# Two window-attention quads in one region of 64x64 products, with the projections of the next quad moved ahead of u and v

## The chip, the cores and the metric

The kernel runs on one core of one Trainium2 chip. The metric is the device time of one execution in microseconds; lower is better. Times of separate executions are compared by their median.

## The reference

The work is the forward and backward pass of windowed self-attention on an image of 256 x 256 tokens with 384 channels, in bf16. The image is cut into 1024 windows of 8 x 8 = 64 tokens, and each window attends only to itself, with a single head over all 384 channels.

```python
qkv = xw @ wqkv                      # xw: (1024, 64, 384)
q, k, v = ...                        # three parts of 384 columns
scale = C ** (-0.5)
p = softmax(einsum('bqc,bkc->bqk', q, k) * scale)
o = einsum('bqk,bkc->bqc', p, v) @ wo
# and with grad_out: the gradients for x, wqkv and wo
```

Inputs are `x`, `wqkv` (384 x 1152), `wo` (384 x 384) and `grad_out`; outputs are the result (`out_0`), the gradient of x (`out_1`), of wqkv (`out_2`) and of wo (`out_3`).

## The kernel before

**Algebra.** The kernel never forms q, k and v. Once, at the start, it multiplies weights: A from the q and k parts (with the scale), B from the v part and wo, and their transposes. After that, for the tokens x and the output gradient g (called `dq` in the code, and `dT` when transposed), it needs four projections: `z` (from g with B), `y` (from x with A), `u` (from x with B, the values that the probabilities average) and `v` (from x with A transposed, for the gradient). Scores and the gradient of the probabilities come from one set of products, `sd`, whose stationary operand is yz.

**Tiling.** Two windows lie on the 128 partitions, and four such pairs make a quad: 512 tokens, 128 quads in all. Every quad goes through these steps:

- `project(a, 0, mo)` and `project(a, 1, mo)` (lines 161 to 173): z and y, three banks each, a bank from three products of 128x128 stationary against 512 columns, evicted by ACT into `yz` (a single buffer). `gather` (lines 175 to 179) copies z, then y, into `zy` on DVE, and `to_tokens` (lines 181 to 184) has SP transpose `zy` by DMA into `tok`.
- `scores(b)` (line 186): 24 products of 64 columns into one PSUM bank, `sd`.
- `soft(b, 0..5)` (lines 198 to 231): softmax and its gradient on DVE, with one exp on ACT (step 2, L212). Step 4 is the last reader of `sd`.
- `uv(b, t, part)` (lines 233 to 241): u and v, eight groups of three products with 384 columns, evicted by ACT.
- `turn(b)` (lines 243 to 259): transposes the two 64x64 matrices of each window on DVE, five instructions. For the first quads and the last one, small products on PE do it.
- `attention(c)` (line 352) calls `attend(c, t)` four times. One `attend` has twelve products in 64x64 mode, in three sets of four that run concurrently on the four quarters of the array: into banks `pw`, `pd`, `pu`, `po`. Their evictions: `Wq` (L294) and `o` (L287) on ACT, `Uq` (L297) on DVE, `d` on DVE or ACT by the table `EV`. A `pd` bank is written by two neighbouring calls, so at t = 0 two of them are taken, and the last one of a quad is the "edge". The results `o` and `d` are stored through POOL's DMA queue.

**Weight gradients.** For every group of three finished quads (`GQ` = 3) there are six items, one for each of two matrices and three row blocks. An item sums over the twelve token blocks of the group and adds the result to `GF_acc` on DVE (L320). An item can be done in two ways. `gf_rows` is a full sum: twelve 128x128 products into one bank `pg`. `gf_halves` is a half sum: 48 products in 64x64 mode into two banks `ph`, cut into twelve slots of four, which `attention` deals out, four behind each `attend`; after twelve slots both banks are added on DVE.

**Order.** The order of instructions on each engine is the order of the program text, written by hand (`manual_schedule`). Tiles, buffers and semaphores are handled by the framework. All PSUM tiles share one ring of eight banks, `ring`; a new tile takes the slot of the tile that was released earliest, and its first product waits for the eviction that released it. `step(c, b, a, ahead)` (line 360) runs three quads at different ages: scores, softmax and u, v of quad b, z and y of quad a = b + 1, a full sum, and then the attention of quad c = b - 1 with one half sum dealt into it. Loads run four quads ahead (`AHEAD`), the DMA transposes of g and x (`load_turn`, L146) two quads ahead; both queues, SP and POOL, work in order.

Of the kernel before, what the change touches and what calls it, by code (L numbers as in the profile page):

```python
# [23 lines left out]
def kernel(  # L24
# [90 lines left out]
    def windows(ap, st, first, count=2):  # L115
        row, col = st["at"]
        return ap[0, row + WIN * first:row + WIN * (first + count), col:col + WIN, :]
# [2 lines left out]
    OTHER = {0: HI, WT: LO}  # L120

    def load_first(st):
        st["xq"] = xq = grp.tile([P, QUAD, C], BF16, tag="xq", name="xq", bufs=2 * GQ + 5)
        st["dq"] = dq = qp.tile([P, QUAD, C], BF16, tag="dq", name="dq", bufs=6)
        for t in range(QUAD):
            (nc.sync, nc.scalar)[t % 2].dma_start(out=dq[:, t, :], in_=windows(grad_out, st, 2 * t))
        nc.sync.dma_start(out=w_sb[:, :, columns(0)], in_=w_in[:, :, columns(0)])
        nc.scalar.dma_start(out=w_sb[:, :, columns(1)], in_=w_in[:, :, columns(1)])
        for t in range(QUAD):
            nc.sync.dma_start(out=xq[:, t, :], in_=windows(x, st, 2 * t))  # L130
        nc.gpsimd.tensor_copy(out=spare[:], in_=dq[:, QUAD - 1, 0:1])

    def load(st):
        st["xq"] = xq = grp.tile([P, QUAD, C], BF16, tag="xq", name="xq", bufs=2 * GQ + 5)
        st["dq"] = dq = qp.tile([P, QUAD, C], BF16, tag="dq", name="dq", bufs=6)
        for t in range(QUAD):
            nc.gpsimd.dma_start(out=dq[:, t, :], in_=windows(grad_out, st, 2 * t))  # L137
        for t in range(QUAD):
            (nc.gpsimd if st["i"] == AHEAD + 1 else nc.sync).dma_start(out=xq[:, t, :], in_=windows(x, st, 2 * t))

    def load_turn(st):
        st["xT"] = qp.tile([P, QUAD, CK, P], BF16, tag="xT", name="xT", bufs=3)
        st["dT"] = qp.tile([P, QUAD, CK, P], BF16, tag="dT", name="dT")
        for src, dst, on_pe in (("dq", "dT", G_ON_PE), ("xq", "xT", X_ON_PE)):
            if st["i"] >= on_pe:
                nc.sync.dma_start_transpose(out=st[dst][:].rearrange("p t m k -> p (t m) k"),  # L146
                                            in_=st[src][:].rearrange("p t c -> p (t c)"))

    def turn_on_pe(st, src, dst):
        for t in range(QUAD):  # L150
# [117 lines left out]
    def attend(st, t):  # L268
        if t == 0:
            st["Uq"] = grp.tile([P, QUAD, C], BF16, tag="Uq", name="Uq")  # L270
            st["Wq"] = grp.tile([P, QUAD, C], BF16, tag="Wq", name="Wq")
        copies = {"A": nc.scalar.copy, "D": nc.vector.tensor_copy}

        def bank(name):
            return ring.tile([P, C], F32, tag="r", name=name)

        def slot(bank, straight, crossed, start=False, stop=False):
            for h in (LO, HI):
                o = OTHER[h.start]
                products = [(h, bank, straight, {"start": True, "stop": True}),  # L280
                            (o, pd[h is LO], crossed, {"start": start, "stop": stop})]
                for o, dst, (lhs, rhs), flags in products if h == LO else products[::-1]:
                    nc.tensor.matmul(dst[o, :], lhsT=operand(st, lhs, t, h), rhs=operand(st, rhs, t, h), **flags)  # L283

        def keep(name, src, i, rows=slice(0, P), sb=None):
            sb = ob.tile([P, C], BF16, tag=name, name=name) if sb is None else sb
            copies[EV[name][i]](out=sb[rows, :], in_=src[rows, :])  # L287
            return sb[rows, :]

        pw = bank("pw")  # L290
        pd = (bank("pd") if t == 0 else st["edge"], bank("pd"))[::-1]
        st["edge"] = pd[0]
        slot(pw, ("Pb", "dq"), ("Pb", "z"), start=True)
        copies[EV["W"][t] if st["i"] >= GQ else "DA"[t % 2]](out=st["Wq"][:, t, :], in_=pw[:])  # L294
        pu = bank("pu")
        slot(pu, ("ST", "xq"), ("dS", "y"))
        copies[EV["U"][t]](out=st["Uq"][:, t, :], in_=pu[:])  # L297
        po = bank("po")
        slot(po, ("PT", "uq"), ("ST", "vq"), stop=True)
        o = keep("o", po, t)  # L300
        above, below = rim.pop("d", None) if t == 0 else None, st["at"][0] + 2 * WIN * QUAD < H
        d = keep("d", pd[1], t, slice(0 if t else WT, P), above)
        nc.gpsimd.dma_start(out=windows(out_0, st, 2 * t), in_=o)  # L303
        if t or above is not None:
            nc.gpsimd.dma_start(out=windows(out_1, st, 2 * t - 1), in_=d if t else above[:])  # L305
        else:
            nc.gpsimd.dma_start(out=windows(out_1, st, 0, 1), in_=d)
        if t == QUAD - 1:
            rim["d"] = sb = ob.tile([P, C], BF16, tag="d", name="d")
            keep("d", pd[0], QUAD, LO, sb)  # L310
            if not below:
                nc.gpsimd.dma_start(out=windows(out_1, st, 2 * QUAD - 1, 1), in_=rim.pop("d")[LO, :])
# [36 lines left out]
                nc.vector.tensor_copy(out=final[f][:, ma, :], in_=GF_acc[:, f, ma, :])  # L349
                yield  # L350

    def attention(st):
        halves = gf_halves(*fill.pop(0)) if fill else iter(())
        for t in range(QUAD):
            attend(st, t)
            yield
            for k in range(QUAD):
                next(halves, None)

    def step(c, b, a, ahead):  # L360

# [40 lines left out]
        for rest in slots:  # L402
            pass

    G_ON_PE, X_ON_PE = 2, 1
    EV = {"z": "AAA", "y": "AAA", "u": "AAAA", "v": "AAAA", "o": "AAAA", "U": "DDDD", "W": "AAAA", "d": "DADAA"}
    quads = [(row, col) for col in range(0, W, WIN) for row in range(0, H, 2 * WIN * QUAD)]
    n = len(quads)
    sts = [{"at": q, "i": i, "on_pe": i <= GQ or i == n - 1} for i, q in enumerate(quads)]
    AHEAD = 4  # L410
    dw_out = out_2.rearrange("(m p) j -> p m j", p=P)
    dwo_out = out_3.rearrange("(m p) n -> p m n", p=P)
# [1 line left out]
    def weight_gradients(group):  # L414
# [19 lines left out]
                copy_out(k, out, pe[:])  # L434

        def rows(name):
            return grp.tile([P, CK, C], BF16, tag="xq", name=name, bufs=2 * GQ + 5)

        for i in range(CK):
            next(group)  # L440
# [26 lines left out]
    with tc.manual_schedule(engines=MANUAL):  # L467
# [5 lines left out]
        load_first(sts[0])  # L473
        load(sts[1])
        load(sts[2])
        load_turn(sts[0])
        load_turn(sts[1])
        load(sts[3])
        load(sts[4])
        turn_blocks(wT[2], w_sb, 2 * CK)  # L480
# [13 lines left out]
        turn_blocks(AT_sb, A_sb)  # L494
        gather(sts[0], 1)
        held = []
        last = None
        get = lambda i: sts[i] if 0 <= i < n else None
        for i in range(n + 1):
            if 0 <= i < n - 2:  # L500
                load_turn(sts[i + 2])
            if 0 <= i < n:
                to_tokens(sts[i])
            step(get(i - 1), get(i), get(i + 1), get(i + AHEAD) if i else None)
            if i > 0:
                held.append(sts[i - 1])
                sts[i - 1] = None
            if held and i == n:
                last = gf_final(held)
            elif len(held) == GQ:  # L510
                fill.extend((held, f, ma) for f in range(2) for ma in range(CK))
                held = []
        while fill:
            gf_rows(*fill.pop(0))
        weight_gradients(last)
# [30 lines left out]
```

## Time and profile before

| what | value |
|---|---|
| median of 3 runs | 1897.86 us (1897.47 to 1898.12) |
| the profiled execution, its own time | 1897.33 us |
| its span, first to last instruction | 1895.6 us |
| granted TensorE clock | 1.0 |
| busy: PE / DVE / ACT / POOL | 1887.7 / 1662.8 / 1523.7 / 862.6 us |
| one steady quad, attention to attention | 14.56 us (905.82 to 920.38) |

In the lines of the profile, "L157" is line 157 of the kernel (the helper that records the products of z, y, u, v, the full sum and the scores, told apart by their tiles pj, pg and sd). PE is the stream of matrix products, PEld the loading of their stationary operands, which overlaps them. A timeline line gives the start and the duration in microseconds, the engine, the line, the operation, the tiles (out <- in), their sizes and how many instructions were merged; in brackets stands the idle time before it and who ended it. A line of the waits gives the engine and line that waited, the one it waited for, the total in microseconds, how many times, and the longest.

### The profile page before, as it was taken

To read this page: it belongs to the slowest core of one execution; us is meant where nothing else is said; L and a number is where in the kernel's file an instruction comes from. 1 tells how busy PE (TensorE), PEld (TensorE's weight loads), DVE (VectorE), ACT (ScalarE), POOL (GpSimd) and SP (SyncE) were. 2 spreads that over 40 slices of the span, in tenths; PEclk is the share of its full clock that TensorE was granted. 3 is DMA by queue.
4 is the path that set the end of the run, shared out by engine and by line. 5 is a ranking of instruction groups with operands and counts; after the bars stand their busy time and mean duration, and the time that the engine had idled before them with its cause. 6 is when DMAs were issued, how large, how long until landed. Compare 5 with 4: busy or idle time off the path is not lost.

```text
span 1895.6 us, 57194 instructions
## 1 busy us (share of the span) xinstructions
PE 1887.7 (100%) x22398; PEld 1125.4 (59%) x22398; DVE 1662.8 (88%) x3602; ACT 1523.7 (80%) x3346; POOL 862.6 (46%) x1576
## 2 busy tenths in 40 slices
PE   9999999999999999999999999999999999999999
PEld 5555565556555655565556555655565566556655
DVE  6888888888888888888888888888888888888887
ACT  7888788878887888788878887888788878887884
POOL 4444444445444444454445444544444445444532
PEclk9999999999999999999999999999999999999999
DMA  9999999999999999999999999999999999999995
GB/s 224 244 212 225 221 211 221 216 221 218 210 222 220 212 224 213 224 215 215 227 215 220 213 218 223 218 208 222 218 222 218 214 222 219 212 213 227 219 183 115
DMA packets 948911, 408.28 MB, mean 215 GB/s; under 512 B 830880, under 2 KB 924064, under 8 KB 948640
## 3 DMA queue, kind: packets, MB, share of 16 engines
q1 hardware_dynamic: 872128, 252.63, 78.2%
q0 software_dynamic: 75264, 151.11, 31.3%
q8 instruction: 175, 2.87, 0.6%
q10 hardware_dynamic: 1248, 0.89, 0.2%
q14 instruction: 96, 0.79, 0.1%
HBM read 101.84 MB, written 101.84 MB: 107 GB/s over the span
## 4 chain that ended last, share of the span: by engine, by line
PE 99%; DVE 1%; ACT 0%; issue 0%; ACTq 0%
PE pj L157 53%; PE pg L157 13%; PE ph L338 13%; PE sd L157 5%; PE pw L283 5%; PE po L283 4%; PE pu L283 4%; PE pd L283 1%; PE pe L427 0%; DVE Uq L297 0%; PE warm L87 0%; PE pc L106 0%; DVE Wq L294 0%; PE pt L99 0%; DVE d L287 0%
## 5 line engine op out<-in xcount | busy, mean ns | idle before, releaser
L303 POOL DMA_DIRECT2D out_dram<-o x512 | 273.6, 534 | 919.3 <-ACT o L287 903.7
L294 ACT CAST Wq<-pw 128x384 bf16<-128x384 f32 x506 | 243.4, 481 | 275.8 <-PE pw L283 275.5
L157 PEld LDWEIGHTS <-xT 128*128 128x128 bf16 x3072 | 291.4, 98 | 182.5
L157 PE MATMUL pj<-B_sb,xT 128*128 128x384 bf16 x1536 | 333.6, 326 | 0.0
L157 PE MATMUL pj<-AT_sb,xT 128*128 128x384 bf16 x1536 | 333.4, 326 | 0.0
L137 POOL DMA_DIRECT2D dq<-in_grad_out_dram x508 | 268.8, 540 | 77.9 <-DMA out_dram<-d 25.2
L297 DVE CAST Uq<-pu 128x384 bf16<-128x384 f32 x512 | 282.8, 552 | 13.8 <-PE pu L283 1.4
L305 POOL DMA_DIRECT2D out_dram<-d x480 | 278.6, 580 | 12.3 <-ACT uq L241 5.1
L157 PE MATMUL pj<-dT,BT_sb 128*128 128x512 bf16 x1152 | 269.6, 379 | 0.1
L157 PE MATMUL pj<-xT,A_sb 128*128 128x512 bf16 x1152 | 269.5, 379 | 0.0
L171 ACT CAST yz<-pj 128x512 bf16<-128x512 f32 x384 | 224.3, 585 | 38.4 <-PE pj L157 29.6
L283 PE MATMUL pd<-tok,ps 64*64 64x384 bf16 x2048 | 254.4, 326 | 0.0
L287 ACT CAST o<-po 128x384 bf16<-128x384 f32 x512 | 250.0, 488 | 1.5 <-PE po L283 1.4
L241 ACT CAST vq<-pj 128x384 bf16<-128x384 f32 x512 | 246.6, 482 | 3.6
L241 ACT CAST uq<-pj 128x384 bf16<-128x384 f32 x512 | 243.7, 476 | 3.7 <-PE pj L157 1.9
L173 ACT CAST yz<-pj 128x512 bf16<-128x512 f32 x384 | 224.7, 585 | 24.5 <-PE pj L157 0.6
L258 DVE STREAM_TRANSPOSE PS<-ps 32x256 bf16<-32x256 bf16 x492 | 214.5, 436 | 9.4
L157 PEld LDWEIGHTS <-xq 128*128 128x128 bf16 x1572 | 153.4, 98 | 115.6 <-issue 0.9
L338 PEld LDWEIGHTS <-xq 64*64 64x64 bf16 x6000 | 175.9, 107 | 67.8
L338 PE MATMUL ph<-Wq,xq 64*64 64x384 bf16 x3984 | 204.2, 323 | 0.0
L157 PEld LDWEIGHTS <-A_sb 128*128 128x128 bf16 x1152 | 112.5, 98 | 135.6
L157 PEld LDWEIGHTS <-BT_sb 128*128 128x128 bf16 x1152 | 112.5, 98 | 122.5
(95 smaller groups left out, 3049.2 us busy)
## 6 DMA issues: line engine op xcount, KB each, us to landing
out_dram<-o POOLq DMA_DIRECT2D x512, 96.0 KB, 3.8
xq<-in_x_dram SPq DMA_DIRECT2D x508, 96.0 KB, 4.0
dq<-in_grad_out_dram POOLq DMA_DIRECT2D x508, 96.0 KB, 5.8
out_dram<-d POOLq DMA_DIRECT2D x480, 96.0 KB, 4.3
out_dram<-d POOLq DMA_DIRECT2D x64, 48.0 KB, 4.8
tok<-zy SPq DMA_TRANSPOSE x128, 7.4
xT<-xq SPq DMA_TRANSPOSE x127, 7.7
dT<-dq SPq DMA_TRANSPOSE x126, 7.7
```

The lines of the kernel that those rows point to most:

```text
L137: nc.gpsimd.dma_start(out=dq[:, t, :], in_=windows(grad_out, st, 2 * t))
L157: nc.tensor.matmul(out, lhsT=lhsT, rhs=rhs, start=start, stop=stop)
L171: ENG[EV["z"][mo]](out=yz[:, mo, :, 0:4:3, :], in_=pj[:])
L173: ENG[EV["y"][mo]](out=yz[:, mo, :, 1:3, :], in_=pj[:])
L241: cp(out=dst[:, t, :], in_=pj[:])
L283: nc.tensor.matmul(dst[o, :], lhsT=operand(st, lhs, t, h), rhs=operand(st, rhs, t, h), **flags)
L287: copies[EV[name][i]](out=sb[rows, :], in_=src[rows, :])
L294: copies[EV["W"][t] if st["i"] >= GQ else "DA"[t % 2]](out=st["Wq"][:, t, :], in_=pw[:])
L297: copies[EV["U"][t]](out=st["Uq"][:, t, :], in_=pu[:])
L303: nc.gpsimd.dma_start(out=windows(out_0, st, 2 * t), in_=o)
L305: nc.gpsimd.dma_start(out=windows(out_1, st, 2 * t - 1), in_=d if t else above[:])
L338: nc.tensor.matmul(dst[o, :], lhsT=st["xq"][h, t, ma * P + o.start:ma * P + o.stop], rhs=st["UW"[f] + "q"][h, t, :], start=(i == 0), stop= ...
```

## The change

Quads 0 to 9 run as before. From quad 10 on, the loop takes two quads at a time (`double(i)`):

- `front(b, a, ...)` runs for each of the two: scores of b, a full sum beside the first softmax steps, then z and y of the next quad a, and only after them u and v of b. In the first front both gathers and the transposition to tokens of a follow at once; in the second they are left for later.
- Then both attentions run one behind the other, each with one half sum dealt out as before. Behind t = 2 and t = 3 of the first attention stand the two gathers of the quad after the pair, and `to_tokens` between the two attentions.
- x of two quads is loaded in the first front, g in each; the transposes of g and x are issued three quads ahead and separately. The x ring has twelve buffers instead of eleven.
- In even quads of the pairs the eviction of `d` at t = 0 goes to ACT instead of DVE.
- The last quad is turned on DVE like the others.

The text of the general case has parameters (`EVEN_ROWS`, `ODD_ROWS`, `EVEN_SETS`), which are all 1 here, so that the branches for no full sum or for two half sums in one attention are taken only where no sums are left.

```diff
--- before.py
+++ after.py
@@ -120,7 +120,7 @@
     OTHER = {0: HI, WT: LO}
 
     def load_first(st):
-        st["xq"] = xq = grp.tile([P, QUAD, C], BF16, tag="xq", name="xq", bufs=2 * GQ + 5)
+        st["xq"] = xq = grp.tile([P, QUAD, C], BF16, tag="xq", name="xq", bufs=2 * GQ + 6)
         st["dq"] = dq = qp.tile([P, QUAD, C], BF16, tag="dq", name="dq", bufs=6)
         for t in range(QUAD):
             (nc.sync, nc.scalar)[t % 2].dma_start(out=dq[:, t, :], in_=windows(grad_out, st, 2 * t))
@@ -130,21 +130,25 @@
             nc.sync.dma_start(out=xq[:, t, :], in_=windows(x, st, 2 * t))
         nc.gpsimd.tensor_copy(out=spare[:], in_=dq[:, QUAD - 1, 0:1])
 
+    def load_dq(st):
+        st["dq"] = dq = qp.tile([P, QUAD, C], BF16, tag="dq", name="dq", bufs=6)
+        for t in range(QUAD):
+            nc.gpsimd.dma_start(out=dq[:, t, :], in_=windows(grad_out, st, 2 * t))
+
+    def load_xq(st):
+        st["xq"] = xq = grp.tile([P, QUAD, C], BF16, tag="xq", name="xq", bufs=2 * GQ + 6)
+        for t in range(QUAD):
+            (nc.gpsimd if st["i"] == AHEAD + 1 else nc.sync).dma_start(out=xq[:, t, :], in_=windows(x, st, 2 * t))
+
     def load(st):
-        st["xq"] = xq = grp.tile([P, QUAD, C], BF16, tag="xq", name="xq", bufs=2 * GQ + 5)
-        st["dq"] = dq = qp.tile([P, QUAD, C], BF16, tag="dq", name="dq", bufs=6)
-        for t in range(QUAD):
-            nc.gpsimd.dma_start(out=dq[:, t, :], in_=windows(grad_out, st, 2 * t))
-        for t in range(QUAD):
-            (nc.gpsimd if st["i"] == AHEAD + 1 else nc.sync).dma_start(out=xq[:, t, :], in_=windows(x, st, 2 * t))
-
-    def load_turn(st):
-        st["xT"] = qp.tile([P, QUAD, CK, P], BF16, tag="xT", name="xT", bufs=3)
-        st["dT"] = qp.tile([P, QUAD, CK, P], BF16, tag="dT", name="dT")
-        for src, dst, on_pe in (("dq", "dT", G_ON_PE), ("xq", "xT", X_ON_PE)):
-            if st["i"] >= on_pe:
-                nc.sync.dma_start_transpose(out=st[dst][:].rearrange("p t m k -> p (t m) k"),
-                                            in_=st[src][:].rearrange("p t c -> p (t c)"))
+        load_dq(st)
+        load_xq(st)
+
+    def load_turn(st, dst):
+        st[dst] = qp.tile([P, QUAD, CK, P], BF16, tag=dst, name=dst, bufs={"xT": 3, "dT": 2}[dst])
+        if st["i"] >= ON_PE[dst]:
+            nc.sync.dma_start_transpose(out=st[dst][:].rearrange("p t m k -> p (t m) k"),
+                                        in_=st[dst[0] + "q"][:].rearrange("p t c -> p (t c)"))
 
     def turn_on_pe(st, src, dst):
         for t in range(QUAD):
@@ -284,7 +288,8 @@
 
         def keep(name, src, i, rows=slice(0, P), sb=None):
             sb = ob.tile([P, C], BF16, tag=name, name=name) if sb is None else sb
-            copies[EV[name][i]](out=sb[rows, :], in_=src[rows, :])
+            ev = EVEN if st["i"] > PAIRED and st["i"] % 2 == 0 and name in EVEN else EV
+            copies[ev[name][i]](out=sb[rows, :], in_=src[rows, :])
             return sb[rows, :]
 
         pw = bank("pw")
@@ -349,13 +354,70 @@
                 nc.vector.tensor_copy(out=final[f][:, ma, :], in_=GF_acc[:, f, ma, :])
                 yield
 
-    def attention(st):
-        halves = gf_halves(*fill.pop(0)) if fill else iter(())
+    def attention(st, sets=1):
+        halves = [gf_halves(*fill.pop(0)) for k in range(min(sets, len(fill)))]
+        slots = (None for part in halves for slot in part)
         for t in range(QUAD):
             attend(st, t)
             yield
-            for k in range(QUAD):
-                next(halves, None)
+            for k in range(QUAD if sets < 2 else QUAD + 2):
+                next(slots, None)
+
+    def front(b, a, rows, gathers):
+        scores(b)
+        soft(b, 0)
+        if rows and fill:
+            soft(b, 1)
+            soft(b, 2)
+            for row in range(rows):
+                gf_rows(*fill.pop(0))
+            z = 0
+        else:
+            z = 2
+            for mo in range(z if a is not None else 0):
+                project(a, 0, mo)
+            soft(b, 1)
+            soft(b, 2)
+        i = b["i"]
+        if a is not None:
+            for mo in range(z, CK):
+                project(a, 0, mo)
+        soft(b, 3)
+        soft(b, 4)
+        soft(b, 5)
+        if i % 2 == 0 and i + AHEAD < n:
+            load_xq(sts[i + AHEAD])
+        if i + AHEAD < n:
+            load_dq(sts[i + AHEAD])
+        if i + 3 < n:
+            load_turn(sts[i + 3], "dT")
+        if a is not None:
+            for mo in range(CK):
+                project(a, 1, mo)
+        if gathers and a is not None:
+            for kind in range(2):
+                gather(a, kind)
+            to_tokens(a)
+        turn(b)
+        if i % 2 == 0 and i + AHEAD + 1 < n:
+            load_xq(sts[i + AHEAD + 1])
+        for t in range(QUAD):
+            for part in range(2):
+                uv(b, t, part)
+        if i + 3 < n:
+            load_turn(sts[i + 3], "xT")
+
+    def double(i):
+        a = sts[i + 2] if i + 2 < n else None
+        front(sts[i], sts[i + 1], EVEN_ROWS, True)
+        front(sts[i + 1], a, ODD_ROWS if a is not None else 2, False)
+        for t, part in enumerate(attention(sts[i], EVEN_SETS)):
+            if t >= 2 and a is not None:
+                gather(a, t - 2)
+        if a is not None:
+            to_tokens(a)
+        for part in attention(sts[i + 1]):
+            pass
 
     def step(c, b, a, ahead):
 
@@ -402,11 +464,14 @@
         for rest in slots:
             pass
 
-    G_ON_PE, X_ON_PE = 2, 1
+    ON_PE = {"dT": 2, "xT": 1}
+    EVEN_ROWS, ODD_ROWS, EVEN_SETS = 1, 1, 1
+    PAIRED = 10
     EV = {"z": "AAA", "y": "AAA", "u": "AAAA", "v": "AAAA", "o": "AAAA", "U": "DDDD", "W": "AAAA", "d": "DADAA"}
+    EVEN = {"d": "AADAA"}
     quads = [(row, col) for col in range(0, W, WIN) for row in range(0, H, 2 * WIN * QUAD)]
     n = len(quads)
-    sts = [{"at": q, "i": i, "on_pe": i <= GQ or i == n - 1} for i, q in enumerate(quads)]
+    sts = [{"at": q, "i": i, "on_pe": i <= GQ} for i, q in enumerate(quads)]
     AHEAD = 4
     dw_out = out_2.rearrange("(m p) j -> p m j", p=P)
     dwo_out = out_3.rearrange("(m p) n -> p m n", p=P)
@@ -434,7 +499,7 @@
                 copy_out(k, out, pe[:])
 
         def rows(name):
-            return grp.tile([P, CK, C], BF16, tag="xq", name=name, bufs=2 * GQ + 5)
+            return grp.tile([P, CK, C], BF16, tag="xq", name=name, bufs=2 * GQ + 6)
 
         for i in range(CK):
             next(group)
@@ -473,8 +538,9 @@
         load_first(sts[0])
         load(sts[1])
         load(sts[2])
-        load_turn(sts[0])
-        load_turn(sts[1])
+        for st in sts[:2]:
+            for dst in ("dT", "xT"):
+                load_turn(st, dst)
         load(sts[3])
         load(sts[4])
         turn_blocks(wT[2], w_sb, 2 * CK)
@@ -494,22 +560,33 @@
         turn_blocks(AT_sb, A_sb)
         gather(sts[0], 1)
         held = []
-        last = None
         get = lambda i: sts[i] if 0 <= i < n else None
-        for i in range(n + 1):
-            if 0 <= i < n - 2:
-                load_turn(sts[i + 2])
-            if 0 <= i < n:
-                to_tokens(sts[i])
+        def done(*quads):
+            for st in quads:
+                held.append(st)
+                sts[st["i"]] = None
+                if len(held) == GQ:
+                    group = held[:]
+                    fill.extend((group, f, ma) for f in range(2) for ma in range(CK))
+                    held.clear()
+
+        for i in range(PAIRED):
+            for dst in ("dT", "xT"):
+                load_turn(sts[i + 2], dst)
+            to_tokens(sts[i])
             step(get(i - 1), get(i), get(i + 1), get(i + AHEAD) if i else None)
-            if i > 0:
-                held.append(sts[i - 1])
-                sts[i - 1] = None
-            if held and i == n:
-                last = gf_final(held)
-            elif len(held) == GQ:
-                fill.extend((held, f, ma) for f in range(2) for ma in range(CK))
-                held = []
+            if i > 0 and i < PAIRED - 1:
+                done(sts[i - 1])
+        for dst in ("dT", "xT"):
+            load_turn(sts[PAIRED + 2], dst)
+        to_tokens(sts[PAIRED])
+        for part in attention(sts[PAIRED - 1]):
+            pass
+        done(sts[PAIRED - 2], sts[PAIRED - 1])
+        for i in range(PAIRED, n, 2):
+            double(i)
+            done(sts[i], sts[i + 1])
+        last = gf_final(held)
         while fill:
             gf_rows(*fill.pop(0))
         weight_gradients(last)
```

## The prediction

> **What bounds the kernel now.** I read the page's busy shares and its chain first, then the waits, then the timelines of PE, DVE and ACT through one step in the middle.
>
> ```profile
> PE 1887.7 (100%) x22398; PEld 1125.4 (59%) x22398; DVE 1662.8 (88%) x3602; ACT 1523.7 (80%) x3346; POOL 862.6 (46%) x1576
> ...
> PE 99%; DVE 1%; ACT 0%; issue 0%; ACTq 0%
> ```
>
> PE is never idle and the chain is PE from end to end. So only two things move the time: PE work that disappears, and a place where PE begins to wait. The PE timeline of one step (start, duration, instruction; t1 and t2 left out):
>
> ```profile
> 903.77 2.11 PE L157 MATMUL pg<-Uq,xq 128*128 128x384 bf16 x12
> 905.82 0.35 PE L283 MATMUL pw<-dq,ps 64*64 64x384 bf16 x1
> ...
> 906.00 0.32 PE L283 MATMUL pu<-xq,PS 64*64 64x384 bf16 x1
> ...
> 909.25 0.32 PE L283 MATMUL pw<-dq,ps 64*64 64x384 bf16 x1
> ...
> 909.59 0.32 PE L283 MATMUL po<-uq,PS 64*64 64x384 bf16 x1
> 909.84 0.88 PE L157 MATMUL sd<-xT,yz 128*128 128x64 bf16 x24
> 910.55 0.65 PE L157 MATMUL pj<-B_sb,xT 128*128 128x384 bf16 x3
> ```
>
> See the borders of the attention region (64x64 products between 128x128 ones). Inside either kind a 384-column product, or a set of four concurrent 64x64 ones, starts every 0.155 to 0.163 us. Into the region, twelve pg products take 2.05 us from start to start where 12 x 0.163 is 1.95 (0.10 lost), and the first set takes 0.18 (0.03 lost). Out of it, po to sd is 0.25 (0.10 lost). A region costs 0.23 us in its borders. The waits show the same places, once per quad:
>
> ```profile
> PEld L283 <- DVE zy L179: 39.0, 123, 0.3
> PEld L157 <- issue: 38.9, 129, 0.3
> ```
>
> Then the evictors, DVE first, ACT second, on the last part of the same region:
>
> ```profile
> 908.05 0.55 DVE L179 COPY zy<-yz 128x1536 bf16<-128x1536 bf16 x1
> 908.66 0.56 DVE L297 CAST Uq<-pu 128x384 bf16<-128x384 f32 x1
> 909.14 0.55 DVE L287 CAST d<-pd 128x384 bf16<-128x384 f32 x1
> 909.60 1.14 DVE L320 TENSOR_TENSOR GF_acc<-ph,GF_acc 128x384 f32<-128x384 f32 x2
> 910.66 0.55 DVE L297 CAST Uq<-pu 128x384 bf16<-128x384 f32 x1
> 911.24 0.88 DVE L203 TENSOR_REDUCE mx<-sd 64x4 f32<-64x256 f32 x2
> ```
>
> ```profile
> 909.64 0.48 ACT L294 CAST Wq<-pw 128x384 bf16<-128x384 f32 x1 [0.27 <-PE pw L283]
> 910.01 0.48 ACT L287 CAST o<-po 128x384 bf16<-128x384 f32 x1
> 910.38 0.85 ACT L287 CAST d<-pd 128x384 bf16<-128x384 f32 x2
> ```
>
> The region's products end at about 909.9, but both evictors work on its banks until 911.2. Today this costs nothing: scores needs one bank, then u and v take one bank every 0.49 us. The backlog of 1.3 us is the number on which this forecast stands.
>
> **The change, part by part.**
>
> *Borders removed.* Quads 10 to 127 make 59 pairs, and attention 9 now follows attention 8 directly: 60 regions fewer. 60 x 0.23 = 13.8 us less PE time. The mix of sums stays (two full sums and two half sums for every two quads, as now), so no other PE work goes; the last quad's 16 small turns on PE are noise (under 0.5 us). The Trainium skill, TensorEngine Tiling (Array Packing), Key Properties, says that changing the tiling mode drains the array; TensorE: Matmul & The Clock Gate, Single matmul latency, gives 166 ns beside the streaming, so two drains would be an estimated 0.33 us and the saving 20 us. The rows' 0.23 stands in my sum.
>
> *Second attention behind the first.* I walk it on a clock with zero at the region's first product (905.82). Without waits the second quad starts at 3.91 (t0 to t2 1.14 to 1.16 each, t3 0.48) and takes seven banks within half a microsecond: three at 3.91 (pw and two pd), pu at 4.07, po at 4.23, two ph at 4.42. The ring has eight banks. In the instruction list of the kernel before, the first product of each bank waits for the eviction that freed its slot, eight allocations back in the order of the releases. So these seven wait for releases 12 to 18 of the first quad.
>
> The first twelve (W, U, o, d of t0 to t2) are done at 3.87: the d row, 909.14 + 0.55. ACT's next: W3 at 4.30 (909.64 + 0.48), o3 at 4.67, its two d at 5.0 and 5.4. On DVE the first gather of the quad after next is placed behind d of t2, ahead of the two GF_acc adds; today it lies before U2, in idle time. A step costs 0.46 to 0.58 from start to start (rows above; ten in 5.3 us, 0.53 mean). With 0.48 for the gather, the adds end at 4.84 and 5.40 (today 4.35 and 4.92), U3 at 5.87, the second gather at 6.35, the next quad's U0 at 6.83.
>
> In the instruction list before, releases after d2 run GF, W3, GF, o3, U3, d3, edge. With it: pw starts at 3.91, the first pd at 4.84, the other at once, pu at 5.40, po at 5.56, ph at 5.87 instead of 4.42. That is 1.45 late. Then the four sets of ph (0.65), pw of t1 at 6.52, and pu of t1 at 6.85 rather than 6.68, behind U0: 0.15 more. Later banks are free in time, as the delay lets ACT and DVE catch up. Sum 1.6 us. If slots are reused by completion (W3, o3, GF, d3, GF, edge), ph starts at 5.42, but po of t1 waits for U0: 1.0 + 0.5 = 1.5. If by the order in the text (GF, GF, W3, U3, o3), the second pd waits for 5.40, po for 5.87: 1.65. The order hardly matters, since the end is set by DVE's queue: d, gather, two adds, U, gather, U. With 0.46 a step that is 1.3, with 0.58 some 2.1. I take 1.6: 59 x 1.6 = 94.4 us, and about 1 us for the pair 8 and 9.
> The Trainium skill, TensorEngine Tiling (Array Packing), PSUM Bottleneck, warns that tiling speeds up TensorE and not the copies out of PSUM. Held strictly, the region would be as long as DVE's queue, 17 steps x 0.53 + 0.58 = 9.6 instead of 7.8 us, and the sum 1.8 a pair; the backlog that the rows allow behind a region today speaks for less.
>
> *d of t0 in even quads from DVE to ACT.* 0.56 us off DVE, 0.48 on ACT, early in the first quad where ACT waits 0.28 for pw anyway. Nothing.
>
> *z, y before u, v; the full sum behind scores.* Same products. A front (scores 0.71, full sum 1.95, z and y 1.94 each, u and v 3.90) is 10.44 us of PE. DVE's chain from mx to the end of turn takes 8.2 us today (911.24 to 919.45), 0.5 of it waiting for exp, which the add of the full sum now fills; the even front adds two gathers, 1.1 us. So even front 9.3 and odd 8.2. Mx of the even front starts 0.6 behind scores (DVE's tail), the odd front makes it good, and turn ends about 1 us before the region. Cover gone would cost 59 us for each microsecond that U0 is late. ACT is free for 2 us in the full sum. Before the region eight u and v evictions at 0.48 run against products at 0.49, so the first quad finds its banks free.
>
> *Queues.* On SP, the x loads of both quads now come in the even front, dT and xT three quads ahead instead of two, and tok of the odd quad stands behind the gathers, with x and xT queued behind it; tok of the next even quad stands behind the second gather of the region. SP's four steps take about 14 us of a 14.6 us quad today, but 731 us of its time (420.4 + 310.9, the two longest waits) is waiting for PE. Every transfer lands 7.4 to 7.7 us after issue and is wanted over 12 us later (tok of the odd quad: issued 2 us before u and v end, wanted a front and an attention later). The twelfth x buffer holds the fullest moment: quads 6 to 17 at the second pair. POOL's g loads move ahead of y and of turn, behind the same stores. All nothing; a late transpose would cost its delay once a pair, 59 us per microsecond.
>
> *Sum.* 1897.3 (the profiled execution: span 1895.6 and 1.7 around it) - 13.8 + 94.4 + 1 = 1978.9; the median lies 0.5 above that execution, so 1979.5.
>
> **The rivals.**
> *Faster, the borders alone:* PE finds the seven banks free, 1897.9 - 13.8 = 1884. It needs the wait to be under 0.23 us a pair, that is the 18th release at 4.65. The rows put the 14th alone at 4.67, so against it stands ACT's own pace. Chance 0.08, for an error in my reading of the bank order.
> *ACT's wait alone:* DVE's queue lets go earlier than I place it (the gathers hide), and only W3 and o3 hold the two pd: 4.67 - 3.91 = 0.76, 59 x 0.76 - 12.8 = +32, 1930. Chance 0.09. For it: DVE overlaps some steps (0.46).
> *DVE bounds the pair:* the 1 us margin ahead of the region is lost to exp coming late behind ACT's tail, and U0 starts late as well; 1 us a pair more gives 2039, half of that 2009. Chance 0.06.
> *No real change:* border and wait cancel (wait 0.17 to 0.30 a pair): 1898. Chance 0.02.
>
> **How the numbers follow.** Forecast 0.75, with 1.3 to 2.0 us a pair: 1962 to 2003. The range runs from ACT's case (its 1930 and a little below) to 2005 and leaves out 0.18. A measurement of this kernel tells 0.2% (3.8 us) from no change. Faster 0.08, same 0.02, slower 0.90 (0.75 + 0.09 + 0.06).
>
> **What would show it.** Right: PE idle by about 95 us, in waits of pd, pu and ph for GF_acc, W and U, all within the second quad of each region; sets out of and into the region half as many (the two PEld rows near 65 times); a first quad as today; DVE running gather, adds, U without a gap. A wait at pw of the first quad or at z (for dT) would make the front or the transfers the cause. PE still at 100% makes the forecast wrong.

## The result: slower by 7.0%

| | before | after |
|---|---|---|
| median of 5 runs each | 1898.12 us (1897.47 to 1899.43) | 2034.66 us (2025.67 to 2037.65) |
| ratio, 95% interval | | 1.0704 [1.0674, 1.0734] |
| span of the profiled execution | 1895.6 us | 2032.9 us |
| mean granted TensorE clock | 1.000 | 0.992 |
| two steady quads | 2 x 14.57 = 29.13 us | 30.90 us (50 of 59 periods) |

The page after, busy shares and chain:

```profile
PE 1947.2 (96%) x22346; PEld 1170.3 (58%) x22346; DVE 1622.5 (80%) x3548; ACT 1584.1 (78%) x3403; POOL 843.1 (41%) x1576
PE 81%; DMA 9%; DVE 7%; issue 1%; SPq 1%; ACT 0%; ACTq 0%; DVEq 0%
```

PE now idles for 4% of the span, and the chain, which was PE alone, leaves it for DVE (7%) and for transfers (9%). The waits name both:

```profile
PE pd L287 <- DMA tok<-zy: 31.4, 15, 4.1
PE pd L287 <- DVE GF_acc L325: 30.4, 46, 0.7
PE pu L287 <- DVE GF_acc L325: 11.0, 46, 0.2
PEld L161 <- issue: 20.9, 70, 0.6
```

The two GF_acc rows were forecast; the transposes of `tok`, 31.4 us in 15 waits, were not. The last row counts the borders out of a region: 70 instead of 129.

The second quad of a region in the timeline of PE (its first product follows pu, po and pw of the first quad without a gap; t2 and t3 left out), and under it DVE over the same time:

```profile
1000.83 0.32 PE L287 MATMUL pw<-dq,ps 64*64 64x384 bf16 x1
1001.82 0.35 PE L287 MATMUL pd<-tok,ps 64*64 64x384 bf16 x2 [0.67 <-DVE GF_acc L325]
...
1002.41 0.32 PE L287 MATMUL pu<-xq,PS 64*64 64x384 bf16 x1 [0.24 <-DVE GF_acc L325]
...
1002.87 0.84 PE L343 MATMUL ph<-Wq,xq 64*64 64x384 bf16 x16
...
1003.88 0.32 PE L287 MATMUL pu<-xq,PS 64*64 64x384 bf16 x1
...
1006.65 0.52 PE L161 MATMUL sd<-xT,yz 128*128 128x64 bf16 x12
```

```profile
1000.15 0.55 DVE L292 CAST d<-pd 128x384 bf16<-128x384 f32 x1
1000.73 0.56 DVE L183 COPY zy<-yz 128x1536 bf16<-128x1536 bf16 x1
1001.21 1.15 DVE L325 TENSOR_TENSOR GF_acc<-ph,GF_acc 128x384 f32<-128x384 f32 x2
1002.27 0.55 DVE L302 CAST Uq<-pu 128x384 bf16<-128x384 f32 x1
1002.74 0.63 DVE L183 COPY zy<-yz 128x1536 bf16<-128x1536 bf16 x1
1003.29 0.54 DVE L302 CAST Uq<-pu 128x384 bf16<-128x384 f32 x1
```

The sequence d, gather, two adds, U, gather, U runs without a gap, and PE starts pd within 0.06 us of the first add's end. From pw to ph it takes 2.04 us where 0.51 is the pace: 1.53 late. A clean region lasts 9.92 us; its products alone need 2 x 3.91 + 0.1 = 7.92. So the wait is 2.0 us a pair. The first quad takes 4.09 of it instead of 3.91, the second 5.82 instead of 4.02. Neither evictor is busy all the while: within the 9.92 us DVE idles for 2.4 us, 1.9 of it in the first quad, and ACT for 1.3. The wait comes from the queue that DVE meets at the border, not from an evictor that is busy throughout.

The 137.3 us of span divide so: 58 periods x 1.77 (30.90 - 29.13) = 103; 28 us more in eight disturbed periods, the first after the change-over among them; the rest, about 6, ahead of the first pair (2.4) and behind the last region (3.7). The 28 us are where `tok` is late: seven waits of 2.03 to 4.14 us in the row above, and one of 2.18 us, which the profile puts down to `DVE zy` although PE starts 0.04 us after a `tok` has landed. SP's queue through an undisturbed stretch:

```profile
567.31 7.97 SPq L187 DMA_TRANSPOSE tok<-zy  x1
575.34 2.64 SPq L141 DMA_DIRECT2D xq<-in_x_dram  x4
578.23 4.64 SPq L150 DMA_TRANSPOSE dT<-dq  x1
583.29 5.06 SPq L187 DMA_TRANSPOSE tok<-zy  x1
588.41 2.52 SPq L141 DMA_DIRECT2D xq<-in_x_dram  x4
```

No gap anywhere. The second `tok` could start when its gathers ended on DVE, at 572.90; it started 10.4 us later, behind x and dT, landed at 590.88 and was wanted at 591.00. Here it was just in time. A `tok` row on SP hides no wait for another engine: some 3000 packets of 256 bytes start within it (median), from its beginning on. Medians over the quads 20 to 119, from the times of the gathers on DVE, of the rows on SP, of the landings and of the first product that reads `tok`:

| `tok` of | data ready to start on SP | start to landing | landing to first use (least) | data ready to first use |
|---|---|---|---|---|
| before, all quads | 8.1 us | 7.4 us | 10.4 us (4.8) | 26.4 us |
| after, even quads | 7.2 | 13.8 | 3.8 (0.04) | 24.3 |
| after, odd quads | 9.2 | 7.1 | 2.3 (0.04) | 18.1 |

So `tok` stood 8 us in SP's queue before the change as well, with 10 us to spare. The new order wants the odd quad's `tok` 8 us sooner, and the even quad's takes twice as long to land. What is left to spare was used up in eight periods, as at 656.54:

```profile
656.54 0.53 PE L287 MATMUL pd<-tok,ps 64*64 64x384 bf16 x2 [3.57 <-DMA tok<-zy]
```

This product takes 0.53 us, not 0.35. Windows cut around the long waits say why (columns: window, its length, busy time and instructions of PE, PEld, DVE, ACT, POOL, then the granted clock, the DMA share, GB/s):

```profile
165.00:650.00 485.00, 470.62 (x5385) 283.24 (x5387) 394.42 (x863) 386.00 (x827) 199.84 (x376) 1.00 1.14 202
650.00:665.00 15.00, 11.43 (x201) 7.27 (x194) 9.95 (x20) 8.66 (x21) 9.02 (x17) 0.89 1.14 230
656.50:657.50 1.00, 0.95 (x12) 0.56 (x16) 0.06 (x1) 0.38 (x1) 0.00 (x0) 0.50 0.86 235
659.50:660.50 1.00, 1.00 (x32) 0.70 (x28) 0.56 (x1) 1.00 (x3) 0.11 (x1) 1.00 1.17 218
```

After this wait the clock is at one half, and a microsecond holds 12 products in place of 32, until about 659.4. So a late transpose is paid twice.

### The profile page after: what moved, and what is told of

Its sections match the earlier page's. It is cut to its first block, busy times and chain, and to the rows that moved or that the text cites. A ratio compares the mean times of both kernels' runs of the same rounds, so it can differ in the third digit from the quotient of the medians.

```text
span 2032.9 us, 56982 instructions
## 1 busy us (share of the span) xinstructions
PE 1947.2 (96%) x22346; PEld 1170.3 (58%) x22346; DVE 1622.5 (80%) x3548; ACT 1584.1 (78%) x3403; POOL 843.1 (41%) x1576
## 4 chain that ended last, share of the span: by engine, by line
PE 81%; DMA 9%; DVE 7%; issue 1%; SPq 1%; ACT 0%; ACTq 0%; DVEq 0%
PE pj L161 43%; PE pg L161 12%; PE ph L343 9%; DMA tok<-zy 8%; PE sd L161 5%; PE pu L287 3%; PE pd L287 3%; DVE GF_acc L325 3%; PE pw L287 2%; PE po L287 2%; DVE zy L183 1%; DVE d L292 1%; DMA xq<-in_x_dram 1%; DVE PS L262 1%; DMA xT<-xq 1%
## 5 line engine op out<-in xcount | busy, mean ns | idle before, releaser
L161 PEld LDWEIGHTS <-xT 128*128 128x128 bf16 x3072 | 299.9, 98 | 209.8
L136 POOL DMA_DIRECT2D dq<-in_grad_out_dram x508 | 273.8, 549 | 195.5 <-DMA out_dram<-d 84.0
L287 PE MATMUL pd<-tok,ps 64*64 64x384 bf16 x2048 | 285.6, 335 | 64.3 <-DMA tok<-zy 31.4
L310 POOL DMA_DIRECT2D out_dram<-d x480 | 258.4, 538 | 70.8 <-DMA out_dram<-o 22.4
L287 PEld LDWEIGHTS <-ps 64*64 64x64 bf16 x3072 | 133.9, 107 | 173.1 <-issue 102.7
L343 PEld LDWEIGHTS <-xq 64*64 64x64 bf16 x5952 | 200.1, 108 | 53.7 <-issue 10.3
L216 ACT ACTIVATE ex<-sh 128x256 f32<-128x256 f32 x128 | 53.3, 417 | 227.5 <-DVE sh L212 227.5
L287 PE MATMUL pw<-dq,ps 64*64 64x384 bf16 x1024 | 215.5, 334 | 1.1 <-DVE Uq L302 1.0
L287 PE MATMUL pu<-xq,PS 64*64 64x384 bf16 x1024 | 196.0, 332 | 11.7 <-DVE GF_acc L325 11.0
```

Source lines behind the costliest of these rows:

```text
L161: nc.tensor.matmul(out, lhsT=lhsT, rhs=rhs, start=start, stop=stop)
L343: nc.tensor.matmul(dst[o, :], lhsT=st["xq"][h, t, ma * P + o.start:ma * P + o.stop], rhs=st["UW"[f] + "q"][h, t, :], start=(i == 0), stop= ...
```

## The experiments

Two theories stood at the start. *Evictions at the border of the two quads*: the seven banks wait for DVE's queue as walked in the prediction, and the late transposes are a second, separate cost. *Order and queues*: z and y ahead of u and v, and the loads that move with them, cost the time, in the front or on SP. "Pair" below is the time of two quads in undisturbed periods, "region" the time from its first 64x64 product to the next 128x128 one.

### Without the shared region

```diff
         front(sts[i], sts[i + 1], EVEN_ROWS, True)
-        front(sts[i + 1], a, ODD_ROWS if a is not None else 2, False)
-        for t, part in enumerate(attention(sts[i], EVEN_SETS)):
-            if t >= 2 and a is not None:
-                gather(a, t - 2)
-        if a is not None:
-            to_tokens(a)
+        for part in attention(sts[i], EVEN_SETS):
+            pass
+        front(sts[i + 1], a, ODD_ROWS if a is not None else 2, True)
```

> Keeps the new order of each front (z and y ahead of u and v, full sum behind scores, transposes three quads ahead), but each quad's attention follows its own front again, so no two attentions touch; both gathers lie in the front. Theory 1 (PE waits for PSUM banks where the second attention follows the first): the wait of 2.0 us a pair is gone and the 59 saved borders with it, so 2034 - 59 x 2.0 + 59 x 0.23 = about 1930 if the late token transposes stay, 1900 if they go too. Rival (the new order of the front or of the loads costs the time): stays near 2030.

1922.48 us, ratio 1.0130 [1.0113, 1.0146]. Every attention has its own region again, and the two gathers and the transpose of the next even quad lie in the front; all else is kept. The quads take 14.57 and 14.76 us in turn, the regions 4.03 and 4.22: 112 of the 137 us are gone, with the order of z, y, u, v and the new loads still in place, and no wait of `pd` for GF_acc is left among PE's waits. The 0.19 is in even quads, the ones whose d of t0 lies on ACT. The same with `EVEN = {}`:

> As apart, with d of t0 of even quads on DVE. Theory: the 0.19 us that every second quad took longer in apart is that copy, so all quads take 14.57 and the total is 1898 plus the change-over at quad 10 (12 us in apart) = 1910. That leaves the new order of the front with no cost of its own in the steady state. Rival (the 0.19 us belongs to the order or the loads): stays at 1922.

1912.05 us, 1.0081 [1.0066, 1.0096], and every steady quad 14.57. So the reordering by itself costs nothing per quad, the moved d costs 0.19 us a pair, and what is left lies at the change-over (two periods of 18.56 and 22.01 us in place of 14.57) and in the last quad, which is turned on DVE:

```profile
PE pd L287 <- DMA tok<-zy: 4.7, 1, 4.7
PE pu L287 <- DVE PS L262: 2.0, 2, 1.4
```

The theory of order and queues fell for the front. Of its transfers one is late even here, where the new order of loads begins. After that SP idles for a fifth of the time: each `tok` starts 0.03 us after its data is ready and lands 10.8 us ahead of its use (medians), and SP's transposes take 1072 us in all, against 1558 in the changed kernel, for the same number of them.

### The parts of the wait inside the region

d of t0 back on DVE, the rest as changed (`EVEN = {}`):

> The d of t0 in even quads goes back to DVE (the table EVEN is empty); all else as in the changed kernel. Theory: on ACT that copy delays o of t1, and po of t2 in the first quad of a region waits 0.16 us for the bank; on DVE it lies in idle time. A clean pair takes 30.7 instead of 30.9 us, the total falls by about 10. Rival (nothing, as the prediction had it): clean pair 30.9.

2030.99 us, 1.0698 [1.0673, 1.0722]; pair 30.77, region 9.80. The pair is 0.13 shorter, on one more DVE step: ACT was the late one. The medians alone do not show it, since their intervals overlap. In the trace of the changed kernel, o of t1 ends on ACT at 1030.36, behind d, and po of t2 starts at 1030.41.

Both gathers out of the region, into the front; the transpose stays where it was:

```diff
-        if gathers and a is not None:
+        if a is not None:
             for kind in range(2):
                 gather(a, kind)
-            to_tokens(a)
+            if gathers:
+                to_tokens(a)
...
-        for t, part in enumerate(attention(sts[i], EVEN_SETS)):
-            if t >= 2 and a is not None:
-                gather(a, t - 2)
+        for part in attention(sts[i], EVEN_SETS):
+            pass
```

> The two gathers leave the shared region and go ahead of turn in the odd front; the token transpose stays where it was. Theory 1, with DVE's queue as what sets the wait: GF_acc, U and the next U come 0.5 to 1.1 us earlier, so a clean pair takes 30.0 to 30.4 instead of 30.9 us, total down by 30 to 55 us. Rival (ACT's pace sets the wait): a clean pair stays at 30.8 to 30.9.

2021.36 us at the median of runs from 1998.82 to 2031.08, ratio 1.0612 [1.0548, 1.0676]; pair 30.36, region 9.38. The pair came as expected, the total did not. Two steps fewer on DVE gave 0.54 a pair: PE's wait at pd for GF_acc fell from 30.4 us to 10.6. But a new wait came in its place: a gather in the front waits for the transpose that still reads `zy`, and U stands behind the gather:

```profile
DVE zy L183 <- DMA tok<-zy: 57.3, 34, 3.8
...
PE pu L287 <- DVE Uq L302: 32.7, 24, 2.7
PE pd L287 <- DVE GF_acc L325: 10.6, 45, 0.8
```

More products in the region, as cover: no full sum in the even front, two half sums in the first attention (`EVEN_ROWS, ODD_ROWS, EVEN_SETS = 0, 1, 2`).

> Same number of sums a pair, but the even quad's full sum becomes a second half sum in the first attention, six sets behind each of its four steps, also behind t = 3 (EVEN_ROWS 0, EVEN_SETS 2). Theory 1: about 1 us of products that need no new bank lies at the border, and 0.3 us more behind each earlier step, so nearly all of the 2.0 us a pair goes: 2034 - 59 x 1.8 = about 1928 with the late transposes still there. Rival (the second attention's products themselves are slow, or its operands late): stays above 2000.

2017.16 us, 1.0638 [1.0614, 1.0661]. In undisturbed pairs 30.02; region 10.99 against 9.86 of products, a wait of 1.1 instead of 2.0, where 0.2 had been expected. The border itself is covered: the waits of pd and pu for GF_acc, 30.4 and 11.0 us in the changed kernel, are gone from PE's list, and in a clean region the second quad follows the first at the pace of the products. What is left stands elsewhere, in steps of 0.2 to 0.4 us from one set to the next where the pace is 0.16: at ph behind t = 2 of the first quad, and at ph, po and pu of the second. Late transposes rose to 63.4 us in 46 waits, so that most pairs show one, and took most of the gain.

Three sets behind each `attend` instead of four, so that a half sum spreads over all four steps of an attention:

```diff
-            for k in range(QUAD if sets < 2 else QUAD + 2):
+            for k in range((QUAD - 1 if st["i"] >= PAIRED else QUAD) if sets < 2 else QUAD + 2):
```

> The changed kernel with the half sum dealt out three sets behind each step instead of four, four and four, so that three also stand behind t = 3, at the border to the second attention; the number of products is the same. Theory 1: half a microsecond of cover moves to the border, but the two adds come after U3 and the second gather on DVE, so some of it is given back: a clean pair 30.3 to 30.6 instead of 30.9, total about 2005 to 2020. Rival (the sum of DVE's and ACT's work in the region sets its length, wherever the cover lies): clean pair 30.8 to 31.0.

2032.55 us, 1.0716 [1.0699, 1.0732]; region 10.21, pair 31.19. The pair is longer than either theory had it. At the border the largest step from one set to the next falls from 0.99 to 0.50 us, but the first quad, which lost 0.18 us to waits as changed, now loses 0.65. So here the cover moved the wait to other banks. That is nearer to the rival, that the region's evictions as a whole set its length, though 31.19 lies above its 31.0 too. A test of the rival takes the half sums out altogether (`EVEN_ROWS, ODD_ROWS, EVEN_SETS = 2, 2, 0`, and no sets in the second attention): no GF_acc at all in the region, and half the products.

> The changed kernel with no half sums in the shared region: each front has two full sums instead of one (EVEN_ROWS 2, ODD_ROWS 2, both attentions with none). The products are the same in number; 3.9 us of them move from the region into the fronts, so without waits the region would be 4.0 and a pair 28.9 us. If the evictions of both attentions set the region's length (ACT 23 x 0.375 = 8.6 us; DVE 13 steps x 0.55 = 7.2, less the 1.3 us that may trail behind the region), the region takes 7.3 to 8.7 us and a clean pair 32.2 to 33.7. If only the burst at the border between the two attentions costs (as the prediction walked it), the wait stays near 2 us: clean pair 30.5 to 31.2.

2118.63 us, 1.1175 [1.1150, 1.1200]; pair 32.83. The region lasts 7.96 us where its products need 3.94. ACT's timeline through it:

```profile
1004.97 0.48 ACT L299 CAST Wq<-pw 128x384 bf16<-128x384 f32 x1
1005.34 0.48 ACT L292 CAST o<-po 128x384 bf16<-128x384 f32 x1
1005.71 0.50 ACT L292 CAST d<-pd 128x384 bf16<-128x384 f32 x1
1006.08 0.51 ACT L299 CAST Wq<-pw 128x384 bf16<-128x384 f32 x1
1006.45 0.53 ACT L292 CAST o<-po 128x384 bf16<-128x384 f32 x1
```

One eviction every 0.37 us with nothing between; 23 of them (16 of W and o, 7 of d) are 8.5 us. With the attention's own evictions alone, two quads in a row are bound by ACT. For the region as changed, where ACT idles for 1.3 us, this is not shown. Put side by side, the wait shrinks as the products grow, and never vanishes:

| kernel | products of the region | region | wait |
|---|---|---|---|
| no half sums | 3.94 us | 7.96 us | 4.0 us |
| as changed | 7.92 | 9.92 | 2.0 |
| three half sums | 9.86 | 10.99 | 1.1 |
| three half sums, d on DVE, no gathers | 9.86 | 10.89 | 1.0 |

### The late transposes

The front's x load and the transposition of g moved behind `turn`, so that they no longer stand on SP ahead of the odd quad's `tok`:

```diff
-        if i % 2 == 0 and i + AHEAD < n:
-            load_xq(sts[i + AHEAD])
...
-        if i + 3 < n:
-            load_turn(sts[i + 3], "dT")
...
         turn(b)
+        if i % 2 == 0 and i + AHEAD < n:
+            load_xq(sts[i + AHEAD])
+        if i + 3 < n:
+            load_turn(sts[i + 3], "dT")
```

> On SP's queue, the first x load and the transpose of g in the even front go behind the token transpose of the odd quad. Theory 2 (that transpose stands too late in SP's queue and lands after PE wants it in some 13 pairs): those waits go, 2034 - 30 = about 2003, and every pair takes 30.9 us. Rival (the transposes are slowed by other traffic, not by their place): stays at 2034 or moves the waits to dT, xT or another tok.

2047.73 us, 1.0788 [1.0771, 1.0804]: slower than the change itself.

```profile
PE pj L161 <- DMA xT<-xq: 24.9, 12, 3.5
PE pd L287 <- DMA tok<-zy: 3.8, 3, 1.9
```

The wait left `tok` and came back at xT, as the rival had it: here the order on SP only chose which transfer is late. Next, less traffic beside it: the stores of `out_0` are left out from the first pair on (8 of the some 17 stores of a pair; this part of the result isn't written).

```diff
-        nc.gpsimd.dma_start(out=windows(out_0, st, 2 * t), in_=o)
+        if st["i"] < PAIRED:
+            nc.gpsimd.dma_start(out=windows(out_0, st, 2 * t), in_=o)
```

> Leaves out the stores of the result out_0 from quad 10 on, eight of the 17 stores of a pair; everything else as in the changed kernel. Theory 2a (the transposes are late because the stores of two attentions and the loads behind them run at the same time): waits for tok fall from 31 us to under 5, the median to about 2000, and a clean pair stays at 30.9. Theory 2b (the order on SP and when its triggers fire make them late): waits for tok stay above 20 us, median above 2020.

2001.65 us, 1.0545 [1.0528, 1.0562].

```profile
PE pd L287 <- DVE GF_acc L326: 39.2, 59, 0.7
PE pu L287 <- DVE GF_acc L326: 14.1, 59, 0.2
PE pd L287 <- DMA tok<-zy: 5.3, 1, 5.3
```

All pairs but the first are now clean, at 30.82, and the only late transpose is the one at the change-over: the excess of disturbed periods fell from 27.7 us to 4.5. With fewer stores beside them the transposes are in time, and `tok` again starts 0.05 us after its data is ready; this shows the second cause and its size, though not which of the transfers delays which.

Both gathers and `to_tokens` in the front (three `tok` buffers, and one softmax buffer to make room):

> Both gathers and the token transpose of the next even quad go into the odd front, 9 us ahead of where the changed kernel issues it; a third tok buffer (paid by single buffers for the small softmax tiles). Theory 2b: with the trigger earlier SP's queue runs with less delay, waits for tok mostly go, and with the gathers out of the region a clean pair takes 30.35: about 1898 + 59 x 1.22 + 10 for the change-over = 1980. Theory 2a: waits for tok stay at 10 us or more (11 in gather_early), median 2000 or above.

2000.39 us, 1.0542 [1.0478, 1.0607]; pair 30.36 and region 9.38, as with the gathers alone; the late transfers are xT (15.0 us in 6) and tok (7.7 in 3). That lies between the two theories, and decides neither.

### All of it together

`tok_early`, three half sums and d on DVE:

> As tok_early, with the even quad's full sum as a second half sum in the first attention, six sets behind each step, and d of t0 on DVE. Theory 1: the border has cover and DVE's queue is shorter by two gathers, so the waits for banks fall from 2.0 to under 0.4 us a pair: clean pair 28.9 to 29.4, total 1895 to 1925 with 10 for the change-over and what is left of late transposes. Rival (something else than banks makes the second attention slow): clean pair above 29.8.

1971.63 us, 1.0407 [1.0358, 1.0456]; pair 29.92. The same with the three-set spread in place of three half sums:

> As tok_early (gathers and token transpose in the odd front, third tok buffer), with three sets behind each step and d of t0 on DVE. Theory 1: cover at the border and a short DVE queue, wait 0.4 to 0.7 us a pair: clean pair 29.3 to 29.6, total 1925 to 1950 with change-over and late transposes. Rival (the region's length is set by the total of evictions): clean pair 29.9 or more, as in combo.

2002.22 us at the median of runs from 1973.78 to 2008.27, too far apart for an interval; pair 30.21. Both had been expected to come under the 29.13 of two separate quads, or near it, and both missed. The best shared pair stays 0.8 us above. In the first, what is late is once more a transfer:

```profile
PE pj L161 <- DMA xT<-xq: 16.5, 8, 4.9
```

No version tried beats the kernel before; the nearest is the one without the shared region, 0.81% slower.

## Where the prediction was right, and where it failed

**Direction and mechanism: right.** Slower at 0.90, by waits of the second quad for its banks. The trace bears out the walk where a wait can be seen: pd starts 0.05 us after the first add, pu 0.05 after the second (1002.36), ph 0.05 after U3 (1002.82); for pw and po it shows no wait of their own.

**Borders: right.** They fell from 129 to 70, and the wait of 2.0 in the region less 0.23 is the measured 1.77 a pair.

**The front: right.** Z and y ahead of u and v cost nothing, shown by the 14.57 us of each quad without the shared region. The rival by which DVE bounds the pair gave times near the measured one (2039 against 2034.66), but by a mechanism that no wait shows: PE waits for the front nowhere in a clean pair. That its number is the nearest is chance. The rivals of free banks and of ACT's wait alone fell with the GF_acc rows.

**The wait in the region: mis-sized, 1.6 against 2.0 us a pair.** The walk itself was close (1.53 against 1.45 up to ph, 0.20 against 0.15 at pu of t1). The larger miss is the step "d of t0 ... Nothing": 0.18 us in the first quad, where a first quad as today had been named a sign of being right. The cover that I named, ACT's wait of 0.28 us for pw, was smaller than the 0.48 that I put there; with d back on DVE the pair gains 0.13. Together 58 x 0.4 = 23 us.
The Trainium skill, TensorEngine Tiling (Array Packing), PSUM Bottleneck, is the warning that I weighed lower. Its strict reading, 9.6 us and 1.8 a pair, is nearer to the 9.92 than my walk. As a formula it does not hold either, since DVE idles for 2.4 us of the region: two DVE steps fewer are 1.06 by it and gave 0.54; one DVE step more, with d moved back, should cost 0.53 and gained 0.12. Both evictors count.

**"All nothing" for the queues: wrong, 28 us.** The failed step is "731 us of its time (420.4 + 310.9, the two longest waits) is waiting for PE". I took those waits as slack, and counted a transfer from its start on SP (7.4 to 7.7 us to landing), with nothing for its time in the queue. In the timeline SP issues back to back, before as after (1807 us of 1896, 1924 of 2033), and a transpose on it mostly lasts 2 to 8 us. The queue put 8.1 us between the data and the start before the change, and 9.2 us for the odd quads after it; with the odd quads' time to first use down from 26.4 to 18.1 us, 2.3 us were left to spare instead of 10.4. I had priced a late transpose in every pair; it was late in a few, up to 4.1 us each, and the clock added to it.

The two misses, 23 + 28 = 51 us, are most of the 55 between 1979.5 and 2034.66; the rest is the 6 us ahead of the pairs and behind them, for which I had allowed 1. (By its own chances the range leaves out 0.08 + 0.02 + 0.06 = 0.16, where the prediction says 0.18; nothing hangs on it.)

## What to carry to other kernels

When two stages are joined to save the change between them, ask what the evictors did during the stage that stood in between: here it hid 1.3 us of backlog, and the join paid 2.0 us to save 0.23. Walk the buffer slots through the joined stage on both evictors, since a step moved to the other one is free only if the idle time there is as long as the step. And count a transfer's slack from the moment its data is ready to its first use, with its time in the queue taken off: the list of waits may call that time waiting for another engine, so read the queue's timeline before calling a transfer hidden.

## What the hardware showed beyond the forecast

**A wait of about 2 us can halve the clock.** The granted clock was 1.0 in the kernel before, up to its last 0.8 us. After, it fell to 0.50 in seven stretches, each around one of the seven long waits for `tok`, of 2.03 to 4.14 us; the waits of about 1.1 us and the eighth long one left it at 1.0. The shortest wait that led to it, and the long one that did not:

```profile
1443.55 0.35 PE L287 MATMUL pd<-tok,ps 64*64 64x384 bf16 x2 [2.03 <-DMA tok<-zy]
1538.62 0.35 PE L287 MATMUL pd<-tok,ps 64*64 64x384 bf16 x2 [2.18 <-DVE zy L183]
```

Windows around three of the seven, the last one around the shortest wait:

```profile
150.00:165.00 15.00, 11.61 (x180) 7.12 (x178) 9.62 (x20) 9.07 (x22) 8.97 (x17) 0.77 1.17 259
1090.00:1104.00 14.00, 9.87 (x177) 6.28 (x173) 7.10 (x14) 8.11 (x20) 6.39 (x12) 0.76 1.13 244
1438.00:1452.00 14.00, 11.97 (x213) 7.71 (x206) 9.79 (x20) 9.28 (x23) 9.35 (x18) 0.88 1.13 229
```

Length times lost clock is 15 x 0.23 = 3.5, 14 x 0.24 = 3.4 and 14 x 0.12 = 1.7 us, and 15.2 over all seven. Part of that falls on the waits themselves; PE was busy for 27.6 us at half clock, so that some 14 of the 28 us of late transposes are this. The trace's clock records give the stretches as 3413 or 6827 ns, and in all 14 traces every change of the clock lies on a grid of 3413 ns, counted from the first record. On that grid (windows at full clock, the first 34 us and the last 20 us of each trace left out), with PE idle for 60% or more of a window the next one ran at half clock, 43 times of 43; with less than 50% idle never, in 7820 windows; in between 8 times of 17. So a wait counts by what it leaves idle within one window: one of 1.97 us (gathers in the front) halved the clock, one of 3.25 us that lay across two windows (three half sums) did not. The Trainium skill, TensorE: Matmul & The Clock Gate, Part 1, tells of a free-running window of 3413 ns and of half clock after one idle window or more. The lengths and the grid agree; but a window idle by 60% was enough here.

**Transposes slow down beside stores.** From issue to landing, `tok` took 7.4 us before, 9.4 after, and 6.4 with the attentions apart and d on DVE. With the `out_0` stores left out `tok` took 7.9 and xT 4.0 where they had been 9.4 and 7.7. Why only eight periods are disturbed, and at irregular places, stays open; so does the last 1.0 us of wait in the best shared region.
